# Earlier casts of global values, deferred normalising in slots 1 to 6 and one Strassen unit less at the end of an attention and expert kernel

## The chip, the cores and the metric

The kernel runs on one core of one Trainium2 chip. The metric is device time of one execution in microseconds (us); the figure for a kernel is the median of several runs. One execution is also recorded by the hardware profiler, and the rows in this document come from that record. PE is TensorE, DVE VectorE, ACT ScalarE, POOL GpSimd and SP the queue of SyncE, which issues transfers.

## The reference, cut to what matters

First an attention over 8 batches, 8 heads, 512 local and 32 global positions of width 64, then a layer of 8 experts over all 4352 rows.

```python
s_g = scale * q_g @ concat(k_g, k_l).T          # global rows see every key
out_g = softmax(s_g) @ concat(v_g, v_l)
s_l = concat(q_l @ k_g.T, where(|i-j| <= 32, q_l @ k_l.T, -1e9)) * scale
out_l = softmax(s_l) @ concat(v_g, v_l)         # local rows: a window and the global keys
x = rows of concat(out_g, out_l)                # 4352 x 512
P = exp(x @ w_gate - max), 8 times normalised over rows and columns
out = sum over e of P[:, e] * (relu(x @ w1[e]) @ w2[e])
```

## The kernel before, in words

Each engine works through its own instructions in the order in which the program issues them; there is no scheduler, so the order of the code is the order on each engine. Instructions wait for semaphores that other engines or transfers raise.

**The start and the slots.** A unit n is a batch b and a pair of heads hp (n = 4b + hp; 32 units). The main loop runs slots s = 0 to 33. In slot s the code issues for unit s the scores in three parts, `st_B(s, 0..2)`: products on PE into a score buffer `sc`, then for each block of 64 rows a masking with a running minimum on DVE (`ms`, `mx`, L379) and an exponential on ACT (`Pu`, L382). For unit s-1 it issues the transposes of the window weights (`st_D1`, `ptw` to `pw`), those of the global weights and of the finished rows of unit s-2 (`st_D2`, `tgx` to `pg` and `xT`), and the products with the values, `st_E(s-1)`. For unit s+1 it issues the transposes of keys and queries (`st_A`, `pk` and `pq`, copied to `kTe` by DVE and to `qpl` or `qbd` by ACT). Below, B(s, p), D1(n) and E(n) stand for these calls.

`st_E(n)` multiplies the window weights with the local values in `va` and `vb` (two layouts of the same values, shifted by 64 rows) and the global weights with the global values in `vgz`, into the buffer `po`. It then normalises on DVE: a reciprocal (`rr`, L427) and a product (`xn`, L428). `po` is a single buffer, shared with the scores of the global rows (`st_G1`, `sg`). Slot 2 issues E(0), slot 3 E(1) and E(2), every later slot E(s-1). The global rows follow in `st_G1` (even slots; a maximum `m` on DVE and an exponential `Pg` on ACT), `st_G2`, `st_G3` and `st_G3n` (odd slots; the last normalises: `rg` and `xgn` on DVE and ACT).

`va` and `vb` have a column of ones behind each head's values, and `va` a pad of zeros. For batches 0 and 1 `va` is filled by four loads on POOL's queue and `vb` by one load and by five copies on POOL (`part`, L204 to L209). `vgz` is zero but for the global values and a column `own`; its values are first cast to a scratch `vg16` in DRAM (`cast_vg`, on POOL's queue) and then spread by four transfers on SP's queue (`load_vz`). Ahead of the first slot `clear` sets pad and ones of `va` and `vb` on DVE, and `clear_z` sets `vgz` and `vgn` on POOL. POOL's queue at the start holds, in this order: the loads of queries and keys (`qs`, `ks`) of batch 0, the mask, the cast of the global values, the loads of `va` and `vb`, the cast for batch 1, `clear_z`, the loads of `qs` and `ks` of batch 1, the five copies into `vb`, the first expert weights.

From slot 5 on PE also makes the first two experts' layers in pieces (`p_l1`, `ph` to `hT`; `p_l2`, `py`). Between the transposes of slots 1 to 4 `keep_busy` issues products that nobody reads; they multiply the identity with `kTe`.

**The experts.** The six other experts run in stages with one level of Strassen's scheme: a `Unit` is 256 rows of the second layer with seven products m1 to m7 of 4 instructions each, 28 of 256 columns, in a buffer `z` of which there are two; its sums of inputs (`sums`, four, on DVE), copies on ACT, and reads `r1`, `r2`, `r7` on DVE that add the result into the output rows. The last stage leaves four units u0 to u3. u0 and u3 are done in the plain way, `plain`: for each half j of the rows eight products of 512 columns, then one read; pieces of other units are issued between them at given points `(j, n)`. u1 and u2 are Strassen units; the sums of u2 are formed on POOL.

Of the kernel before, what the change touches and what calls it, by code (L numbers as in the profile page):

```python
# [10 lines left out]
FP16 = mybir.dt.float16  # L11
FP32 = mybir.dt.float32
AF = mybir.ActivationFunctionType
ALU = mybir.AluOpType
# [9 lines left out]
def kernel(  # L24
# [13 lines left out]
    nc = tc.nc  # L38

    B, H, Sl, Dh = q_l.shape  # L40
# [3 lines left out]
    P = 128  # L44
# [5 lines left out]
    NJ = Sl // P  # L50
    HP = H // 2
    DP = D // P
    FT = F // P
# [4 lines left out]
    VW = Dh + 1  # L58
# [10 lines left out]
    ones_f = persist.tile([P, P], FP32)  # L69
    identity = persist.tile([P, P], FP16)  # L70
# [58 lines left out]
    with ExitStack() as att:  # L129
        att_c = att.enter_context(tc.tile_pool(name="att_c", bufs=1))  # L130
        att_in = att.enter_context(tc.tile_pool(name="att_in", bufs=2))
        att_wk = att.enter_context(tc.tile_pool(name="att_wk", bufs=2))
# [45 lines left out]
        def load_vz(b):  # L178
            for i in range(4):
                nc.sync.dma_start(out=vgz[b % 2][i:P:4, i, :, 0:Dh], in_=vg16[b])  # L180

        def cast_vg(b):
            nc.gpsimd.dma_start(out=vg16[b], in_=v_g[b].rearrange("h g d -> g h d"))

        def load_v(b):
            va, vb = vab[b % 2]
            vz = vgz[b % 2]
            src = v_l[b].rearrange("h s d -> s h d")

            def first():  # L190
                if b != 1:
                    cast_vg(b)
                nc.gpsimd.dma_start(out=va[W:P, 0, :, 0:Dh], in_=src[0:96])

            def mid(j):
                nc.gpsimd.dma_start(out=va[:, j, :, 0:Dh], in_=src[P * j - W : P * j + 96])

            def last():
                r = HB if natural(b) else W
                nc.gpsimd.dma_start(out=vb[r : r + W, NJ - 1, :, 0:Dh], in_=src[Sl - W : Sl])  # L200

            def part(eng, lo):
                if lo:
                    eng.tensor_copy(out=vb[96:P, NJ - 1], in_=va[W : 2 * W, 0])  # L204
                    eng.tensor_copy(out=vb[0:HB, 0:2], in_=va[HB:P, 0:2])
                    eng.tensor_copy(out=vb[0:HB, 2:NJ], in_=va[HB:P, 2:NJ])
                else:
                    eng.tensor_copy(out=vb[HB:P, 0:2], in_=va[0:HB, 1:3])
                    eng.tensor_copy(out=vb[HB:P, 2], in_=va[0:HB, 3])  # L209

            def move():
                if natural(b):
                    return part
                nc.sync.dma_start(out=vb[96:P, NJ - 1], in_=va[W : 2 * W, 0])
                nc.sync.dma_start(out=vb[0:W, :], in_=va[HB : HB + W, :])
                nc.sync.dma_start(out=vb[HB : HB + W, :], in_=va[HB + W : P, :])
                nc.sync.dma_start(out=vb[W:HB, 0 : NJ - 1], in_=va[0:W, 1:NJ])
                nc.sync.dma_start(out=vb[HB + W : P, 0 : NJ - 1], in_=va[W:HB, 1:NJ])
                load_vz(b)

            return [first] + [lambda j=j: mid(j) for j in range(1, NJ)] + [last, move]
# [38 lines left out]
        def run(steps):  # L260
            for f in steps:
                f()
# [14 lines left out]
        steps = load_qk(0, 2, 4, H)  # L277
# [12 lines left out]
        def clear(i, eng):  # L290
            va, vb = vab[i]
            eng.memset(va[0:W, 0], 0.0)
            eng.memset(va[:, :, :, Dh:VW], 1.0)
            eng.memset(vb[:, :, :, Dh:VW], 1.0)

        def clear_z(i, eng):
            eng.memset(vgr[i].bitcast(mybir.dt.uint32), 0)
            eng.tensor_copy(out=vgz[i][:, :, :, Dh], in_=own.unsqueeze(2).to_broadcast([P, 4, H]))
            if i == 0:
                eng.memset(vgn[0 : P - Sg], 0.0)  # L300
                eng.memset(vgn[P - Sg : P, :, Dh:VW], 1.0)

        clear(0, nc.vector)
        clear(1, nc.vector)
        for t in range(2):
            (nc.vector.tensor_copy if t else nc.scalar.copy)(out=staged[0][t][:, 0:2], in_=fh[t])
        for a in range(2):
            band = mask[HB * a : HB * (a + 1), 1, 0:KW]
            for base, m, c in ((0, -1, 1), (2 * W, 1, -1)):
                nc.gpsimd.affine_select(out=band, in_=band, compare_op=ALU.is_ge, fill=NEG, base=base,  # L310
                                        pattern=[[c, KW]], channel_multiplier=m)
        run(steps[2:4])
        *steps, move = load_v(0)
        part = move()
        run(steps)
        cast_vg(1)
        clear_z(0, nc.gpsimd)
        load_vz(0)
        nc.sync.dma_start(out=vgn[P - Sg : P, :, 0:Dh], in_=vg16[0])

        st = {}
# [63 lines left out]
        def st_D1(n):  # L385
            d = st[n]
            ptw = ps_tr.tile([P, NHB, P], FP16, tag="tr")
            for i in range(NHB):
                nc.tensor.transpose(ptw[:, i, :], d["Pu"][:, i // 4, 0:KW, i % 4], identity)  # L389
            d["pw"] = att_wk.tile([P, NHB, P], FP16, tag="pw", name="pw")  # L390
            nc.vector.tensor_copy(out=d["pw"], in_=ptw)
# [18 lines left out]
        def st_E(n):  # L410
            b, hp = divmod(n, HP)
            d = st[n]
            vz = vgz[b % 2]
            d["xn"] = att_wk.tile([P, NJ, P], FP16, tag="xn", name="xn")
            po = ps_po.tile([P, NJ, 256], FP32, tag="po")
            for j in range(NJ):
                for a in range(2):
                    for first in (True, False):
                        for par in range(2):
                            i, h = 2 * j + par, 2 * hp + a  # L420
                            lhs, rhs = (d["pw"][:, i], vab[b % 2][par][:, j, h, :]) if first else \
                                (d["pg"][:, i // 4], vz[:, i % 4, h, :])
                            nc.tensor.matmul(po[HB * par : HB * (par + 1), j, VW * a : VW * (a + 1)],  # L423
                                             lhs[:, HB * a : HB * (a + 1)], rhs, start=first, stop=not first)
            pv = po[:, :, 0 : 2 * VW].rearrange("p j (a v) -> p j a v", a=2)
            rr = att_wk.tile([P, NJ, 2], FP32, tag="rr2", name="rr2")
            nc.vector.reciprocal(out=rr, in_=pv[:, :, :, Dh])  # L427
            nc.vector.tensor_tensor(out=d["xn"].rearrange("p j (a v) -> p j a v", a=2), in0=pv[:, :, :, 0:Dh],  # L428
                                    in1=rr.unsqueeze(3).to_broadcast([P, NJ, 2, Dh]), op=ALU.mult)

        gs = {}

# [117 lines left out]
        def keep_busy(n):  # L550
            pm = ps_mm.tile([P, 512], FP32, tag="mm", name="pm")
            for i in range(n):
                nc.tensor.matmul(pm, identity, kTe[0][:, 0:512], start=True, stop=True)

        queue = []
        NU = B * HP
# [5 lines left out]
        def permuted_masks():  # L562
            for i in (3, 2):
                nc.vector.tensor_copy(out=mask[:, i, 0:KW].rearrange("q (y x w) -> q x y w", x=2, w=W),
                                      in_=mask[:, 1, 0:KW].rearrange("q (x y w) -> q x y w", x=2, w=W))
            nc.vector.memset(mask[:, 2, 3 * W : KW], NEG)
        st_A(0)
        unread(2, 256)
        first_keys()
        for s in range(NU + 2):  # L570
# [66 lines left out]
            f1("a")  # L637
            if s < NU:
                st_B(s, 0)
            if even:  # L640
                st_G1(*divmod((s - 2) // 2, 2))
            if 1 <= s <= NU:
                st_D1(s - 1)
            if s == 3:
                st_E(1)
            if g_odd:
                st_G2(gb, gg)
            f2("a")
# [10 lines left out]
            if s < 7:  # L659
                st_A(s + 1)  # L660
            if 1 <= s < 5:
                keep_busy(3)
            if s == 4:
                st_D2(None, 1)
            if s == 1 or s == 2:
# [7 lines left out]
            if s + 1 < NU and s >= 7:  # L673
                st_A(s + 1)
            if s == 2:
                st_E(0)
            if 3 <= s <= NU:
                st_E(s - 1)
            if g_odd:
                st_G3(gb, gg)  # L680
            f2("a")
            if g_odd:
                st_G3n(gb, gg)
            if s == 6:
                f1("v")
# [75 lines left out]
    with tc.tile_pool(name="tpool", bufs=2) as tpool, \  # L761
# [90 lines left out]
        class Unit:  # L852
# [6 lines left out]
            def o(self, j):  # L859
                return acc_of(self.m)[:, self.c[j], :]  # L860

            def sums(self, eng=nc.vector):
                a11, a12, a21, a22 = self.a
                s = self.s = hsum.tile([P, 3, HF, P], FP16, tag="hs", name="hs")
                for o, x, y, op in ((s[:, 1], a11, a21, ALU.subtract), (a21, a21, a22, ALU.add),
                                    (s[:, 0], a21, a11, ALU.subtract), (s[:, 2], a12, s[:, 0], ALU.subtract)):
                    eng.tensor_tensor(out=o, in0=x, in1=y, op=op)  # L867

            def mm(self, o, lhs, rhs, first):
                for fk in range(HF):  # L870
# [247 lines left out]
            w()  # L1118
        u0, u1, u2, u3 = final
        u1.sums()  # L1120
        plain(u0, False, {(0, FT - 2): (x.m3, x.r1, lambda: u2.sums(nc.gpsimd)), (1, 3): (u1.m1,)})
        for w in (u1.m7, u1.m2, u1.m6, u2.m1, u1.m4, u1.m5, u1.r2, u1.r7, u2.m7, u2.m2, u2.m6, u1.m3, u1.r1):
            w()
        plain(u3, True, {(0, 3): (u2.m4, u2.m5, u2.r2, u2.r7), (0, FT - 2): (u2.m3, u2.r1)})


# [28 lines left out]
```

## Time and profile before

| | us |
|---|---|
| runs of the kernel before | 996.26, 996.98, 997.41 |
| median | 996.98 |
| profiled execution | 996.39 |
| its span, first to last instruction | 994.6 |

| stretch of the profiled execution, us | PE busy | DVE busy | ACT busy | POOL busy | granted clock |
|---|---|---|---|---|---|
| 0 to 10 | 6.48 | 7.64 | 4.90 | 9.04 | 1.00 |
| 10 to 20 | 8.56 | 8.37 | 8.93 | 9.68 | 0.83 |
| 20 to 30 | 7.91 | 7.55 | 7.31 | 9.76 | 1.00 |
| 30 to 40 | 7.61 | 7.90 | 9.94 | 9.70 | 1.00 |
| 40 to 50 | 9.76 | 9.11 | 8.85 | 2.35 | 1.00 |
| 50 to 60 | 9.56 | 8.12 | 9.62 | 9.87 | 1.00 |
| 60 to 70 | 10.00 | 7.33 | 8.41 | 0.53 | 1.00 |
| 980 to 995 | 9.04 of 15 | 9.13 | 1.07 | 1.88 | 0.97 |

Each row is a window of the record with the busy time of each engine in it. A granted clock of 1.00 is TensorE at full speed. Slot 2 ends near 22 us, slot 3 near 28, slot 4 near 35, slot 5 near 43, slot 6 near 50.

### The profile page before, as it was taken

Reading aid. Unit: us, or ns where it says so; the run is one execution under the profiler, and the core shown is the slowest. Engines: PE = TensorE matmul, PEld = TensorE weight load, DVE = VectorE, ACT = ScalarE, POOL = GpSimd, SP = SyncE. Lnnn points to the kernel's source line nnn. Section 1 sums busy time; section 2 is a strip of 40 time slices with the busy share of each in tenths; the row PEclk is TensorE's granted clock in tenths of the full one; section 3 lists DMA queues with packets and bytes.
Section 4 is the critical chain, followed back from the end, with each engine's and each line's share of the span. In section 5 each row is a group of like instructions: output and inputs, shape, how many; then the busy total and the mean of one; then the engine's idle time right before and its main releaser. Section 6 shows DMA issues by size and latency. Waiting matters only on the chain.

```text
span 994.6 us, 22109 instructions
## 1 busy us (share of the span) xinstructions
PE 978.8 (98%) x8644; PEld 637.0 (64%) x8644; DVE 776.9 (78%) x1919; ACT 659.8 (66%) x1372; POOL 305.2 (31%) x366
## 2 busy tenths in 40 slices
PE   7899999999999999999999999999999999999997
PEld 5565556555555556666666666676767676766765
DVE  7876666666663755899999888997899999888887
ACT  6898888888884566765555555557765555555551
POOL 9649887887860201111111111101111111100001
PEclk9999999999999999999999999999999999999999
DMA  9999999999952477554443333575654543123043
GB/s 165 189 163 207 226 213 212 224 203 234 225 141 85 121 229 189 161 138 118 117 106 75 75 74 75 138 212 138 160 138 118 117 116 71 38 56 73 2 106 128
DMA packets 138248, 138.65 MB, mean 139 GB/s; under 512 B 56800, under 2 KB 110240, under 8 KB 136096
## 3 DMA queue, kind: packets, MB, share of 16 engines
q0 software_dynamic: 105696, 87.32, 51.6%
q1 hardware_dynamic: 31888, 49.60, 15.7%
q8 instruction: 67, 1.10, 0.4%
q10 hardware_dynamic: 560, 0.33, 0.1%
q14 instruction: 37, 0.30, 0.1%
HBM read 144.46 MB, written 39.58 MB: 185 GB/s over the span
## 4 chain that ended last, share of the span: by engine, by line
PE 93%; DVE 2%; ACT 2%; POOL 1%; DMA 1%; issue 1%; SPq 0%; ACTq 0%; DVEq 0%; POOLq 0%
PE z L871 30%; PE pa L969 18%; PE py L537 12%; PE ph L523 11%; PE pb L969 9%; PE pc L969 4%; PE sc L375 1%; PE po L423 1%; PE ptw L389 1%; ACT Pu L382 1%; PE pk L332 1%; DMA vgz<-vg 1%; PE tgx L399 1%; PE pq L332 1%; PE sg L455 0%
## 5 line engine op out<-in xcount | busy, mean ns | idle before, releaser
L871 PEld LDWEIGHTS <-hs 128*128 128x128 f16 x2320 | 226.1, 98 | 96.1 <-issue 2.9
L871 PE MATMUL z<-w2e,hs 128*128 128x256 f16 x1336 | 200.4, 273 | 2.3 <-DVE o L905 1.0
L871 PE MATMUL z<-v,hs 128*128 128x256 f16 x984 | 147.6, 273 | 0.0
L892 ACT COPY z<-z 128x256 f32<-128x256 f32 x100 | 35.7, 357 | 145.9 <-PE z L871 145.9
L523 PE MATMUL ph<-xT,w1e 128*128 128x512 f16 (+1 forms) x576 | 130.2, 367 | 0.6 <-ACT xT L407 0.6
L537 PE MATMUL py<-w2e,hT 128*128 128x512 f16 x544 | 128.2, 379 | 0.0
L382 ACT ACTIVATE Pu<-ms,mx 128x160 f16<-128x160 f32 x256 | 119.6, 637 | 11.7 <-DVE mx L379 9.6
L969 PEld LDWEIGHTS <-w1e 128*128 128x128 f16 x960 | 87.1, 98 | 51.6 <-issue 1.0
L969 PE MATMUL pa<-t,s 128*128 128x512 f16 x384 | 114.2, 379 | 0.0
L787 POOL DMA_DIRECT2D w1e<-in_moe_w_dram x24 | 17.4, 733 | 290.7 <-PE pa L969 220.4
L379 DVE CUSTOM_DVE_ANT_0 ms<-sc,mask 128x160 f32<-128x160 f32 x256 | 70.0, 320 | 46.3 <-ACT yst L540 27.6
L867 DVE TENSOR_TENSOR hs<-hs 128x512 f16<-128x512 f16 x228 | 99.1, 435 | 8.4
L905 DVE SCALAR_TENSOR_TENSOR oy<-z,lg,oy 128x512 f32<-128x512 f32 x128 | 95.8, 748 | 7.3 <-ACT oy L910 5.9
L787 POOL DMA_DIRECT2D w2e<-in_moe_w_dram x24 | 19.8, 830 | 243.6 <-PE z L871 214.2
L973 DVE CUSTOM_DVE_ANT_0 hx<-pb,s 128x512 f16<-128x512 f32 x96 | 65.9, 686 | 36.4 <-ACT s L1003 30.4
L523 PEld LDWEIGHTS <-w1e 128*128 128x128 f16 x576 | 54.5, 98 | 53.0 <-issue 1.1
L989 ACT ACTIVATE hs<-pa 128x512 f16<-128x512 f32 x96 | 57.2, 596 | 46.8 <-PE pa L969 46.8
L973 DVE CUSTOM_DVE_ANT_0 hs<-pb,s 128x512 f16<-128x512 f32 x96 | 65.8, 686 | 24.1 <-ACT s L1003 23.7
L969 PEld LDWEIGHTS <-s 128*128 128x128 f16 x720 | 65.6, 98 | 28.5 <-issue 0.3
L537 PEld LDWEIGHTS <-hT 128*128 128x128 f16 x544 | 49.9, 98 | 51.9
L528 DVE TENSOR_SCALAR hT<-ph 128x512 f16<-128x512 f32 x58 | 40.1, 691 | 50.1 <-PE ph L523 50.0
L526 ACT ACTIVATE hT<-ph 128x512 f16<-128x512 f32 (+1 forms) x86 | 50.7, 589 | 27.6 <-PE ph L523 27.1
(203 smaller groups left out, 1935.0 us busy)
## 6 DMA issues: line engine op xcount, KB each, us to landing
ys<-yd SPq DMA_DIRECT2D x68, 256.0 KB, 3.2
yd<-yst SPq DMA_DIRECT2D x16, 1024.0 KB, 6.4
pw<-in_moe_w_dram POOLq DMA_DIRECT2D x24, 512.0 KB, 10.1
kept<-psum POOLq DMA_DIRECT2D x24, 512.0 KB, 4.8
s<-kept POOLq DMA_DIRECT2D x12, 768.0 KB, 8.8
v<-kept POOLq DMA_DIRECT2D x12, 768.0 KB, 8.7
w1e<-in_moe_w_dram POOLq DMA_DIRECT2D x12, 512.0 KB, 5.4
w2e<-in_moe_w_dram POOLq DMA_DIRECT2D x12, 512.0 KB, 6.5
```

The lines of the kernel that those rows point to most:

```text
L379: nc.vector.tensor_tensor_reduce(out=ms[:, ii, :], in0=sc[:, SW * ii : SW * (ii + 1)], in1=mask[:, mi, :], scale=-scale, scalar=BIG, op0=A ...
L382: nc.scalar.activation(out=d["Pu"][:, i // 4, :, i % 4], in_=ms[:, ii, :], func=AF.Exp, scale=-1.0, bias=d["mx"][:, i : i + 1])
L523: nc.tensor.matmul(ph[:, 0:n], wts[e][0][:, dk, P * fm : P * (fm + 1)], xT[:, dk, c0 : c0 + n], start=(dk == 0), stop=(dk == DP - 1))
L526: nc.scalar.activation(out=hT[:, fm, 0:n], in_=ph[:, 0:n], func=AF.Relu)
L528: nc.vector.tensor_scalar(out=hT[:, fm, 0:n], in0=ph[:, 0:n], scalar1=0.0, scalar2=None, op0=ALU.max)
L537: nc.tensor.matmul(py, hT[:, fk, P * c : P * (c + 1)], wts[e][1][:, fk, :], start=(fk == 0), stop=(fk == FT - 1))
L867: eng.tensor_tensor(out=o, in0=x, in1=y, op=op)
L871: nc.tensor.matmul(o, lhs[:, fk, :], rhs[:, fk, :], start=(first and fk == 0), stop=(fk == HF - 1), skip_group_check=True)
L905: nc.vector.scalar_tensor_tensor(out=o, in0=z, scalar=p, in1=o, op0=ALU.mult, op1=ALU.add)
L969: nc.tensor.matmul(o, lhs[:, dk, P * f : P * (f + 1)], rhs[:, dk], start=(first and n == 0 and dk == 0), stop=(dk == HD - 1), skip_group_c ...
L973: nc.vector._custom_dve(TENSOR_ADD_SAT, out=self.to(i, j), in0=self.of(ps), in1=self.of(s), s0=BIG, s1=0.0)
L989: nc.scalar.activation(out=self.to(1, 0), in_=self.of(self.pa), func=AF.Relu)
```

## The change

- The cast of the global values of batch 0 (`cast_vg(0)`) is issued ahead of the second pair of loads of `qs` and `ks`. The zeroing of `vgz[0]` moves from POOL to DVE. `clear_z(0)`, now without that zeroing, stands behind the first load of `va`; the rest of `va` and `vb` and the cast for batch 1 follow. `clear(0)` and `clear(1)` move from DVE to POOL, behind those loads.
- `st_E` returns its normalising as a function. In slots 2 to 5 it is kept in `later` and issued in the next slot behind B(s, 0), so that the maskings of the first scores stand ahead of it on DVE; E(1) is normalised at once. In slots 3 and 5 `st_G3n` is kept the same way. In slots 4 and 6 D1(s-1) stands ahead of `st_G1`.
- `keep_busy` issues six products of 256 columns with a tile of ones (`ones_f`, read as 16-bit numbers) in place of three of 512 columns with `kTe[0]`.
- u2 is a plain unit: its sums on POOL go, and the second half of u1 is issued between the products of u2.

```diff
@@ load_v(b), first()
-                if b != 1:
+                if b > 1:
                     cast_vg(b)
...
         def clear_z(i, eng):
-            eng.memset(vgr[i].bitcast(mybir.dt.uint32), 0)
+            if i:
+                eng.memset(vgr[i].bitcast(mybir.dt.uint32), 0)
             eng.tensor_copy(out=vgz[i][:, :, :, Dh], in_=own.unsqueeze(2).to_broadcast([P, 4, H]))
...
-        clear(0, nc.vector)
-        clear(1, nc.vector)
+        nc.vector.memset(vgr[0].bitcast(mybir.dt.uint32), 0)
...
+        cast_vg(0)
         run(steps[2:4])
         *steps, move = load_v(0)
         part = move()
-        run(steps)
+        steps[0]()
+        clear_z(0, nc.gpsimd)
+        run(steps[1:])
+        load_vz(0)
         cast_vg(1)
-        clear_z(0, nc.gpsimd)
-        load_vz(0)
+        clear(0, nc.gpsimd)
+        clear(1, nc.gpsimd)
         nc.sync.dma_start(out=vgn[P - Sg : P, :, 0:Dh], in_=vg16[0])
@@ st_E(n)
-            pv = po[:, :, 0 : 2 * VW].rearrange("p j (a v) -> p j a v", a=2)
-            rr = att_wk.tile([P, NJ, 2], FP32, tag="rr2", name="rr2")
-            nc.vector.reciprocal(out=rr, in_=pv[:, :, :, Dh])
-            nc.vector.tensor_tensor(out=d["xn"]..., in0=pv[:, :, :, 0:Dh], ..., op=ALU.mult)
+            def normalise():
+                (the same four statements)
+            return normalise
@@ keep_busy(n)
-                nc.tensor.matmul(pm, identity, kTe[0][:, 0:512], start=True, stop=True)
+                nc.tensor.matmul(pm[:, 0 : 2 * P], identity, ones_f.bitcast(FP16), start=True, stop=True)
@@ the loop over slots
             if s < NU:
                 st_B(s, 0)
+            for f in later:
+                f()
+            later = []
+            if s in (4, 6):
+                st_D1(s - 1)
             if even:
                 st_G1(*divmod((s - 2) // 2, 2))
-            if 1 <= s <= NU:
+            if 1 <= s <= NU and s not in (4, 6):
                 st_D1(s - 1)
             if s == 3:
-                st_E(1)
+                st_E(1)()
...
             if 1 <= s < 5:
-                keep_busy(3)
+                keep_busy(6)
...
             if s == 2:
-                st_E(0)
+                later.append(st_E(0))
             if 3 <= s <= NU:
-                st_E(s - 1)
+                later.append(st_E(s - 1))
+            if s > 5:
+                run(later)
+                later = []
             if g_odd:
                 st_G3(gb, gg)
             f2("a")
-            if g_odd:
+            if g_odd and s in (3, 5):
+                later.append(lambda gb=gb, gg=gg: st_G3n(gb, gg))
+            elif g_odd:
                 st_G3n(gb, gg)
@@ the end
-        plain(u0, False, {(0, FT - 2): (x.m3, x.r1, lambda: u2.sums(nc.gpsimd)), (1, 3): (u1.m1,)})
-        for w in (u1.m7, u1.m2, u1.m6, u2.m1, u1.m4, u1.m5, u1.r2, u1.r7, u2.m7, u2.m2, u2.m6, u1.m3, u1.r1):
+        plain(u0, False, {(0, FT - 2): (x.m3, x.r1), (1, 3): (u1.m1,)})
+        for w in (u1.m7, u1.m2, u1.m6):
             w()
-        plain(u3, True, {(0, 3): (u2.m4, u2.m5, u2.r2, u2.r7), (0, FT - 2): (u2.m3, u2.r1)})
+        plain(u2, False, {(0, 3): (u1.m4, u1.m5, u1.r2, u1.r7), (1, 3): (u1.m3, u1.r1)})
+        plain(u3, True, {})
```

## The prediction

> **What bounds the kernel now.** Read in this order: the page's busy shares and its chain; the chain of the first 30 us; POOL's timeline up to 21 us; the landing of its loads; the clock by microsecond; DVE's and ACT's timelines around 43 us; PE's waits at the end. All numbers are of one execution of 996.39 us (span 994.6 us). The median of the three runs is 996.98 us, 0.59 us more. A measurement of this kernel tells about 0.2%, or 2 us, from no change.
>
> ```profile
> PE 978.8 (98%) x8644; PEld 637.0 (64%) x8644; DVE 776.9 (78%) x1919; ACT 659.8 (66%) x1372; POOL 305.2 (31%) x366
> PE 93%; DVE 2%; ACT 2%; POOL 1%; DMA 1%; issue 1%; SPq 0%; ACTq 0%; DVEq 0%; POOLq 0%
> ```
>
> PE is the bound. From 59.4 us to 980 us it has no gap that counts, so nothing there moves; only the first 59 us and the last 15 us can. What a part of the start gains or loses in front of the first dense stretch of PE comes out at the end one for one.
>
> ```profile
> 12.30 0.33 POOL vgz L298
> ...
> 14.61 6.71 DMA vgz<-vg
> ...
> 21.36 0.53 PE po L423 x21
> ```
>
> Columns: start, length, what. The chain of the start is POOL's queue, then the transfer of the global values into vgz, then unit 0's products E(0) in slot 2.
>
> ```profile
> 13.15 0.78 POOL L174 DMA_DIRECT2D qs<-in_q_l_dram  x1
> ...
> 16.20 0.61 POOL L204 COPY vb<-va 32x520 f16<-32x520 f16 x1
> ...
> 18.97 1.05 POOL L208 COPY vb<-va 64x1040 f16<-64x1040 f16 x1
> 19.96 0.61 POOL L209 COPY vb<-va 64x520 f16<-64x520 f16 x1
> ```
>
> POOL never idles here. E(0) starts on PE at 20.35, 0.33 us after the copy of L208 that fills the half of vb it reads first, and then waits 0.64 us for vgz. So two things stand level in front of E(0): the transfer of vgz and POOL's copies into vb. E(0) ends at 21.87.
>
> ```profile
> va<-in_v_l_dram POOLq DMA_DIRECT2D x1, 128.0 KB, 7.0
> vb<-in_v_l_dram POOLq DMA_DIRECT2D x1, 32.0 KB, 6.4
> ```
>
> The last column is us from issue to landing: the last load of va (issued 9.04) lands at 16.0, that of vb (9.90) at 16.3.
>
> **Part 1, the start.** vg's cast is issued at 4.4 instead of 5.9, and vgz's ones need POOL only for 0.33 us (L298), at about 7.5. The transfers to vgz can leave at some 10.5 instead of 12.65, and land some 2 us sooner: the 0.64 us wait goes. DVE gives up six memsets (2.50 to 4.33, 1.8 us) for one of 128x1040, by L279 (384 elements, 0.38) about 1.0 us. That is at most 0.2 us, since the first key cast then waits for its load; it is worth nothing in front of E(0), which waits for POOL.
>
> What is late next is POOL. The six memsets of va and vb stand on POOL behind the loads of va and vb. In the changed program as built, the memset of va's ones column waits for all four loads of va, and the next one for vb's load. Before, they ran on DVE at 3 us with nothing to wait for. POOL's new order: vg 0.66, qs 0.77, ks 0.75, first va 0.79, L298 0.33, vgn memsets 0.61 and 0.13, three va 2.65, vb 0.75, vg of b=1 0.59, and va's pad memset at the 0.61 of L300; from 4.37 that ends at about 13.1. Then it waits. The queue of transfers is full from 6 to 21 us (landings follow each other 0.3 to 1.9 us apart) and nothing ahead of va's last load goes away, so it lands about when it did: 16.0 to 16.4. Bounds: 15.2 (issued 10.3, with the 4.9 us of the quickest load of that size) and 17.3 (7.0 us again). I take 16.4. Four column memsets at 0.2 (between the 0.13 of L301 and the 0.33 of L298) and a second pad at 0.61 end at 17.8. Queued behind are four loads (3.05 us) and the five copies: they start at 17.8 where they started at 13.15, 4.65 us later. L208 ends at 24.7, L209 at 25.2, E(0)'s last products 0.3 us after that: 25.5 against 21.87. **+3.7 us** (+2.2 to +5.1 by the two bounds). DVE and ACT have nothing else to do then. The later loads have cover: qs and ks of b=1 land at about 24 and are needed some 29; the first w1e is issued 5 us later but had landed 9 us before its use.
>
> PE idles over 4 us there. The clock says what that costs:
>
> ```profile
> 10.00:11.00 1.00, 0.29 (x12) 0.30 (x12) 0.87 (x4) 1.00 (x4) 1.00 (x2) 0.98 1.88 175
> 12.00:13.00 1.00, 1.00 (x16) 0.63 (x14) 0.95 (x4) 1.00 (x3) 0.94 (x3) 0.50 2.74 150
> ```
>
> First number behind the length: PE's busy time; third from the right: granted clock. After three thin microseconds (0.48, 0.35, 0.29) the clock is 0.50 from 11 to 14.4, and ptw's eight transposes take 1.04 us instead of 0.64. In slot 3 some 1.6 us of PE work (rest of E(0), first scores, E(1), G2) lies on the path; part of it would run at half clock. **+0.3 us**, bounds 0 and 1.6. The Trainium skill (TensorE: Matmul & The Clock Gate, Part 1: The HAM clock gate) says that one idle window of about 3.4 us halves the clock until a busy window has passed; by it the whole 1.6 us would double and the sum below would be 1.3 us more. The row agrees in depth and length, though here PE was thin and not idle.
>
> **Part 2, scores ahead of normalising.** No work is added; DVE's order changes, so gaps decide.
> - Slot 3: before, unit 0's normalising (0.9 us) runs right behind E(0), and E(1), which shares the one po buffer, follows at once (22.90). Now three maskings (0.74) come between, and E(1) with all behind it on PE starts later. ACT's idle 1.18 us before its exponentials shrinks by 0.8, but the slot's second maskings go from 3.07 us behind E(0) to 3.5. +0.45.
> - Slot 4: first scores wait for ACT's qpl copy (27.83); DVE idles for them with the normalising queued behind. ACT does the exponentials earlier, then waits for Pg, whose maximum comes behind normalising. Both cancel: 0.05. Slot 5: 0.1, ACT being full.
> - Slot 6 is the dear one:
>
> ```profile
> 42.60 0.56 DVE L494 TENSOR_SCALAR xgn<-pog,rg 32x64 f16<-32x64 f32 x2
> 43.19 0.69 DVE L528 TENSOR_SCALAR hT<-ph 128x512 f16<-128x512 f32 x1
> 43.91 0.32 DVE L379 CUSTOM_DVE_ANT_0 ms<-sc,mask 128x160 f32<-128x160 f32 x1
> ```
>
> Normalising (41.56 to 43.16) fills the time in which PE makes ph. Moved behind the scores it leaves DVE idle until ph is there (42.6) and adds its 1.6 us after 44.25. G1 waits for po until 45.1, the maximum ends at 47.3 instead of 45.5, Pg follows, and ACT's next exponentials start at about 48.1 instead of 46.43. From there ACT is full until PE waits for it at 58.1. +1.6.
>
> Sum **+2.2 us**. If the gaps of ACT (1.18, 0.84 and 0.81 us) were filled and nothing waited, it would be -1.5; if the pad, pw and G1 waits all add up, +3.0. I take the walk, the nearest to the rows.
>
> **Part 3, unread products.** Six of 256 columns for three of 512: 0.81 us on PE as before. They no longer wait for kTe, which in slot 3 costs PE 0.70 us (25.70 to 26.40). ACT hides it: its queue (Pu, pg, xT, qpl) is busy to 27.83 and takes the next exponentials only then. 0; without that cover -0.7.
>
> **Part 4, the last units.**
>
> ```profile
> PE z L871 <- DVE o L905: 1.0, 1, 1.0
> PE z L871 <- DVE oy L905: 1.0, 1, 1.0
> PE z L871 <- DVE ox L905: 0.3, 1, 0.3
> ```
>
> These are PE's waits from 980 to 990. Measured between issues they are 1.12 (980.54 to 981.66), 0.48 and 1.14 us: 2.74. u2 as a plain unit costs 16 products of 512 at 0.216, 3.46 us, for 28 of 256 at 0.109, 3.05: +0.4. Its first three products cover ACT's copy that u1.m4 waits for; five and three cover r2 and r7 up to 0.1 us. u2's sums leave POOL, and u1's four on DVE go from 4.45 us to 1.7 (0.42 each elsewhere), so x.r1 comes early. The stores stay on SP, and the last goes out after the same three pieces of u3. -2.74 + 0.4 + 0.1 = **-2.2 us** (-2.7 if no wait is left, -1.4 if two of 0.4 us are).
>
> **Sum.** 3.7 + 0.3 + 2.2 + 0 - 2.2 = +4.0: 1000.4 for such an execution, and with the 0.6 us to the median 1001.0.
>
> **Rivals.**
> - *Faster:* POOL's wait is short. Then vgz is what mattered: -0.65 at E(0), -1.0 of ACT's gaps, -2.2 at the end: 996.98 - 3.9 = 993.1. It decides if the last load of va has landed by about 12 us, for then L208 ends by 20.4. For it: the chain names vgz. Against it: the load is issued at 10.3, and 4.9 us is the quickest of its size. 0.13.
> - *No change:* the wait is as I say, but the new order fills ACT's gaps (-1.5) instead of costing 2.2: 3.7 + 0.3 - 1.5 - 2.2 = +0.3, 997.3. For it: ACT's waits for mx (4.9 us in 60). Against it: the walk of slot 6. 0.14.
> - *Slower still:* the half clock covers slot 3, 1.6 us where I took 0.3: 1002.3. This is the rule of the page named above. 0.13.
> - That a part does not do what it says: vgz does land sooner, but only the copies are waited for; this is in the forecast.
>
> **How the numbers follow.** The forecast has 0.60, with a range of its own of 998.5 to 1003.0. Slower: 0.60 + 0.13, and 0.01 of the second rival's spread; same: 0.11 of it; faster: 0.13 and 0.02 of it. The range 996.0 to 1003.8 leaves out the faster rival and the far end of the stall's upper bound.
>
> **What would show it.** POOL idle for 2 to 4 us from about 13 us in front of the memset of va; PE idle 4 us in front of E(0), which ends near 25.5; a clock of 0.5 near 25 to 28; the first dense py near 65.5 instead of 59.4; PE's three waits at the end gone. I am wrong if POOL shows no such wait, if E(0) ends before 23, or if the first py comes less than 4 us later.

## The result

The changed kernel takes 1005.19 us (median; 1004.91 to 1007.39) where the kernel before takes 996.98 on the same chip: 8.2 us more, a ratio of 1.0087 [1.0073, 1.0101]. The forecast was 1001.0, with a range up to 1003.8. The sign was right; the loss is twice the one forecast and lies outside the range. The profiled execution took 1005.11 us, its span 1003.3 (994.6 before).

The page of the changed kernel, its busy shares and the shares of its chain:

```profile
PE 983.8 (98%) x8644; PEld 639.8 (64%) x8644; DVE 773.4 (77%) x1913; ACT 659.6 (66%) x1370; POOL 301.1 (30%) x367
...
PE 94%; ACT 2%; POOL 1%; DVE 1%; DMA 1%; issue 0%; POOLq 0%; DVEq 0%; ACTq 0%
```

PE is busy for 5.0 us more with as many products: twelve more unread ones, each of half the size, and twelve fewer in u2, each of twice the size; u2 adds 0.4 us, the unread ones nothing. Most of the 5.0 us is probably the lower clock: in the first 35 us it is 0.50 for some 17 us, against 3.4 us before, and E(0) takes 1.17 us there, for 0.63 in a kernel below that meets it at full clock. The rest of the 8.7 us is waiting. The chain of waits of the first 30 us (start, length, what) says where the first part is:

```profile
8.27 1.65 POOL va L196 x2
9.92 8.17 DMA va<-in_v_l_dram
...
25.11 1.06 POOL vb L208
26.21 1.17 PE po L427 x28
```

Before, vgz stood in this chain ahead of E(0). Now it is va's last load, issued at 9.92 and landing 8.17 us later, and then POOL's copies. POOL's timeline (start, length, what; in brackets idle time before it and what ended that):

```profile
12.15 0.52 POOL L292 MEMSET va<- 32x520 f16 x1
18.18 0.25 POOL L293 MEMSET va<- 128x32 f16 x1 [5.50 <-DMA va<-in_v_l_dram]
...
22.34 0.61 POOL L204 COPY vb<-va 32x520 f16<-32x520 f16 x1
...
25.11 1.05 POOL L208 COPY vb<-va 64x1040 f16<-64x1040 f16 x1
26.10 0.62 POOL L209 COPY vb<-va 64x520 f16<-64x520 f16 x1
```

POOL stands for 5.50 us at the memset of va's ones column, and the four loads of queries and keys and the five copies stand behind it. The copy of L208 ends at 26.2, 6.1 us later than before. In the waits of PE up to 70 us (engine, tile and line, what it waited for; us in total, times, longest) the same stall and a second kind of wait stand first:

```profile
PE po L427 <- POOL vb L208: 4.1, 1, 4.1
PE sg L462 <- DVE xn L434: 2.7, 2, 1.4
```

The first is E(0); PE was there at 21.9, did its first product and waited 4.1 us. The second is `st_G1` in slots 4 and 6, waiting for a normalising that now stands behind the maskings. The clock by microsecond (PE's busy time first behind the length, granted clock third from the right):

```profile
24.00:25.00 1.00, 0.00 (x0) 0.00 (x0) 0.00 (x0) 0.00 (x0) 1.00 (x2) 0.50 1.11 131
...
28.00:29.00 1.00, 0.94 (x8) 0.67 (x8) 0.89 (x7) 0.52 (x2) 1.00 (x3) 0.50 0.92 68
...
30.00:31.00 1.00, 1.00 (x34) 0.93 (x33) 0.41 (x2) 0.00 (x0) 1.00 (x2) 0.50 1.10 195
```

PE idles at 24 us, and the clock stays at 0.50 from 24 to 34 us, through all of slot 3. DVE's timeline in slot 6, which answers to the three lines around 43 us before:

```profile
51.47 0.69 DVE L535 TENSOR_SCALAR hT<-ph 128x512 f16<-128x512 f32 x1 [0.98 <-PE ph L530]
52.65 0.32 DVE L383 CUSTOM_DVE_ANT_0 ms<-sc,mask 128x160 f32<-128x160 f32 x1 [0.49 <-PE sc L379]
...
53.63 0.69 DVE L434 TENSOR_TENSOR xn<-po,rr 128x512 f16<-128x512 f32 x1
...
54.43 0.56 DVE L501 TENSOR_SCALAR xgn<-pog,rg 32x64 f16<-32x64 f32 x2
```

DVE idles 0.98 us for ph, which the normalising used to cover, and does the normalising behind the maskings. At the end, PE's timeline has u1's second half between the products of u2, and then the rest of u2 and u3 in one piece:

```profile
993.06 1.89 PE L958 MATMUL zp<-w2e,hs 128*128 128x512 f16 x8
994.86 0.60 PE L889 MATMUL z<-w2e,hs 128*128 128x256 f16 x4
995.29 4.74 PE L958 MATMUL zp<-w2e,hs 128*128 128x512 f16 x37
```

No line of these carries a wait, and PE's list of waits from 979 us to the end is empty.

To put the time in its place, the first maskings of some blocks serve as marks. T(s, p) is the start of the first masking of B(s, p) on DVE:

| us | E(0) ends | T(3,1) | T(4,1) | T(5,1) | T(6,1) | T(8,0) | T(8,0) to the end |
|---|---|---|---|---|---|---|---|
| before | 21.9 | 24.9 | 31.9 | 37.5 | 46.1 | 59.2 | 935.4 |
| after | 27.4 | 32.3 | 40.3 | 46.4 | 56.5 | 69.9 | 933.4 |

The start and slots lose 10.7 us. From T(8,0) to the end the kernel gains 2.0.

### The profile page after: what moved, and what is told of

Its sections match the earlier page's. It is cut to its first block, busy times and chain, and to the rows that moved or that the text cites. A ratio compares the mean times of both kernels' runs of the same rounds, so it can differ in the third digit from the quotient of the medians.

```text
span 1003.3 us, 22100 instructions
## 1 busy us (share of the span) xinstructions
PE 983.8 (98%) x8644; PEld 639.8 (64%) x8644; DVE 773.4 (77%) x1913; ACT 659.6 (66%) x1370; POOL 301.1 (30%) x367
## 4 chain that ended last, share of the span: by engine, by line
PE 94%; ACT 2%; POOL 1%; DVE 1%; DMA 1%; issue 0%; POOLq 0%; DVEq 0%; ACTq 0%
PE z L889 30%; PE pa L987 18%; PE py L544 12%; PE ph L530 11%; PE pb L987 9%; PE pc L987 4%; PE po L427 2%; PE sc L379 1%; PE ptw L393 1%; PE zp L958 1%; PE pk L336 1%; DMA va<-in_v_l_dram 1%; ACT Pu L386 1%; PE tgx L403 1%; PE pq L336 1%
## 5 line engine op out<-in xcount | busy, mean ns | idle before, releaser
L889 PEld LDWEIGHTS <-hs 128*128 128x128 f16 x2292 | 223.3, 98 | 93.4 <-DVE hs L885 1.2
L889 PE MATMUL z<-w2e,hs 128*128 128x256 f16 x1320 | 198.0, 273 | 0.0
L386 ACT ACTIVATE Pu<-ms,mx 128x160 f16<-128x160 f32 x256 | 119.6, 636 | 16.7 <-DVE mx L383 14.4
L885 DVE TENSOR_TENSOR hs<-hs 128x512 f16<-128x512 f16 x228 | 96.6, 424 | 8.7 <-DVE hs L885 0.5
```

The costliest lines, as they stand in the source:

```text
L386: nc.scalar.activation(out=d["Pu"][:, i // 4, :, i % 4], in_=ms[:, ii, :], func=AF.Exp, scale=-1.0, bias=d["mx"][:, i : i + 1])
L885: nc.vector.tensor_tensor(out=o, in0=x, in1=y, op=op)
L889: nc.tensor.matmul(o, lhs[:, fk, :], rhs[:, fk, :], start=(first and fk == 0), stop=(fk == HF - 1), skip_group_check=True)
```

## The experiments

The theory: the end gains 2.2 us; the moved clears lose 3 to 6 us by making POOL wait for va's last load; the new order loses 2 to 5; the tile of ones is worth nothing. The rivals: that the new order only lost time because the late start made slot 3 slow; that the early transfers to vgz, not the clears, delay E(0); that the half clock is the larger part. First each of the four parts by itself on the kernel before, which took 997.86 in these four comparisons. Differences in us are between medians; the ratios have their 95% intervals.

**The end alone.**

```diff
-        plain(u0, False, {(0, FT - 2): (x.m3, x.r1, lambda: u2.sums(nc.gpsimd)), (1, 3): (u1.m1,)})
+        plain(u0, False, {(0, FT - 2): (x.m3, x.r1), (1, 3): (u1.m1,)})
...
+        plain(u2, False, {(0, 3): (u1.m4, u1.m5, u1.r2, u1.r7), (1, 3): (u1.m3, u1.r1)})
+        plain(u3, True, {})
```

> Before with only the end changed (u2 plain). Theory A: the three waits of PE at the end (2.74 us between issues) go for 0.4 us more of products, -2.0 to -2.2 us, all of it from 980 us on. Rival B: part of the waits comes back as a wait of u1.m3 for r7 or of u3 for a score buffer, -1.4 us or less. The start shows no difference in either.

Measured: 995.29, ratio 0.9972 [0.9961, 0.9984], 2.6 us less. Within the interval this part does what it was costed at.

**The start alone.**

```diff
-                if b != 1:
+                if b > 1:
...
-        clear(0, nc.vector)
-        clear(1, nc.vector)
+        nc.vector.memset(vgr[0].bitcast(mybir.dt.uint32), 0)
...
+        cast_vg(0)
...
+        clear(0, nc.gpsimd)
+        clear(1, nc.gpsimd)
```

> Before with only the start changed (cast sooner, zeroing on DVE, clears on POOL behind the loads). Theory A: POOL waits 5 to 6 us for va's loads, E(0) ends near 27.4 as in the changed kernel, and slot 3 runs at half clock: +6.5 to +8.5 us. Rival B: the half clock costs little when the order of slots 3 to 6 is the old one, so that only the shift of E(0) is left: +5 to +5.8 us. Rival C: the stall of E(0) is taken up by later gaps: under +3 us.

Measured: 1002.84, ratio 1.0046 [1.0033, 1.0059], 5.0 us more. POOL's timeline and, below it, the first of PE's waits up to 32 us:

```profile
18.98 0.25 POOL L293 MEMSET va<- 128x32 f16 x1 [6.34 <-DMA va<-in_v_l_dram]
```

```profile
PE po L427 <- POOL vb L208: 5.1, 1, 5.1
```

The wait is there without any other part. Behind T(3,1) every step of the slots has its old length (7.0, 5.6, 8.5 and 13.0 us to T(8,0)), so a late start does not by itself make the later slots slow. The half clock lasts from 23.5 to 30.3 us here, and what it costs is small: E(0) takes 1.16 us, and E(0) to T(3,1) 3.35 instead of 3.07. Theory A's 6.5 us and more did not come; the 5.0 us are the low end of rival B.

**The order alone.** `st_E` returns its normalising, kept in `later`; D1 ahead in slots 4 and 6; `st_G3n` kept in slots 3 and 5.

```diff
+            for f in later:
+                f()
+            later = []
+            if s in (4, 6):
+                st_D1(s - 1)
...
-                st_E(0)
+                later.append(st_E(0))
```

> Before with only the order changed (scores ahead of normalising, st_D1 ahead of st_G1). Theory A: DVE waits for ph in slot 5 with normalising queued behind, and Pg comes late in slot 6: +1.5 to +2.5 us, of which +1.6 lies in slot 6. Rival B: ACT's gaps in slots 3 to 5 are filled, and the order costs only where the clock is halved: -0.5 to -1.5 us.

Measured: 1002.38, ratio 1.0054 [1.0035, 1.0074], 4.5 us more, about twice what theory A allowed. One line of PE's timeline, and below it the same wait in PE's list of waits of the kernel before (up to 60 us):

```profile
31.95 0.40 PE L458 MATMUL sg<-kTe,qgT 64*32 64x480 f16 x8 [1.29 <-DVE xn L430]
```

```profile
PE sg L455 <- DVE xn L428: 0.4, 1, 0.4
```

`st_G1` of slot 4 stands 1.29 us for the normalising that shares its buffer, 0.4 before, and PE's queue stands behind it. T(3,1) to T(4,1) takes 7.8 us instead of 7.0, all at a clock of 1.00. T(4,1) to T(5,1) takes 6.4 instead of 5.6, but there the clock is 0.50 from 34.4 to 37.8 us. The loss needs no late start.

**The tile of ones alone.**

```diff
-                nc.tensor.matmul(pm, identity, kTe[0][:, 0:512], start=True, stop=True)
+                nc.tensor.matmul(pm[:, 0 : 2 * P], identity, ones_f.bitcast(FP16), start=True, stop=True)
...
-                keep_busy(3)
+                keep_busy(6)
```

> Before with only the unread products changed (a tile of ones, six of 256 columns). Theory A: the wait of PE for kTe in slot 3 (0.70 us) goes but ACT's queue sets the next step: -0.2 to +0.2 us. Rival B: the wait was on the path: -0.7 us. Rival C: half of the ones tile is zero as 16-bit numbers and the products are shorter, so that the clock falls more often: a lower granted clock between 10 and 30 us and +0.5 us or more.

Measured: 998.0, ratio 1.0001 [0.9992, 1.0009]. The times show nothing, but they leave room for 0.8 us, and the trace has a gain: PE's wait for kTe in slot 3 is gone, and T(3,1) to T(4,1) takes 6.5 us instead of 7.0, with every later step as before.

The parts add to 5.0 + 4.5 + 0.1 - 2.6 = 7.0 us; together they measured 8.2. Next, what in the start costs, with a kernel before at 997.05. The edits of the next three are shown against the start alone.

**The start with the clears left on DVE.**

```diff
         nc.vector.memset(vgr[0].bitcast(mybir.dt.uint32), 0)
+        clear(0, nc.vector)
+        clear(1, nc.vector)
...
-        clear(0, nc.gpsimd)
-        clear(1, nc.gpsimd)
```

> The start of the changed kernel, but the clears of va and vb stay on DVE ahead of the first cast; everything else of before. Theory A: the whole loss of the start is POOL's wait for va's loads; without it the copies into vb end at 20 us or sooner, the transfer to vgz has landed, and E(0) ends at 21 to 21.5: -0.3 to -1.0 us against before. Rival B: the earlier transfer to vgz or the 1.0 us zeroing on DVE costs as well: 0 to +2 us.

Measured: 997.6, ratio 0.9999 [0.999, 1.0008]. POOL's timeline:

```profile
17.38 1.05 POOL L206 COPY vb<-va 64x1040 f16<-64x1040 f16 x1 [0.35 <-DMA va<-in_v_l_dram]
18.49 1.05 POOL L208 COPY vb<-va 64x1040 f16<-64x1040 f16 x1
```

The loss is gone. But the early cast brings nothing either: E(0) starts at 21.4 us, 1.9 after L208's copy ends, with no wait for POOL and none for vgz. What stands ahead of E(0) on PE in slots 0 to 2 sets it.

**The clears on POOL, ahead of va's first load.**

```diff
         run(steps[2:4])
+        clear(0, nc.gpsimd)
+        clear(1, nc.gpsimd)
         *steps, move = load_v(0)
...
         cast_vg(1)
-        clear(0, nc.gpsimd)
-        clear(1, nc.gpsimd)
```

> The start of the changed kernel with the clears on POOL, but ahead of va's first load; everything else of before. Theory A: it is the landing that POOL waits for, not the work of the six memsets; POOL does them in about 1.9 us without a wait and has the zeroing of vgz (1.0 us) less, so the copies into vb end 0.9 to 1.5 us later than before: +0.3 to +1.2 us. Rival B: the memsets themselves, or the later loads, cost what the start cost: +4 us or more.

Measured: 997.1, ratio 0.9998 [0.9989, 1.0007]. POOL does the same six memsets, and in the time they cost nothing that shows: it is their place behind the loads, not the work, that costs the 5 us. The copy of L208 comes 0.9 us later than before (19.90 against 18.97) and E(0) starts at 21.4 all the same.

**The start with the cast in its old place.** The clears stay on POOL behind the loads; the transfers to vgz leave at 12.18 us, near the 12.65 of before, instead of 8.2 to 9.0.

```diff
-                if b > 1:
+                if b != 1:
...
-        cast_vg(0)
         run(steps[2:4])
```

> The start alone with the cast of the global values back in its old place behind qs and ks; clears on POOL behind the loads as in the changed kernel. It tells what makes va's last load land at 18.1 us and not at 16.0. Theory A: the five transfers of 32 KB to vgz and vgn, which now leave at 8 to 11 us, run beside va's loads; with the late cast they leave at 12.5, va's last load lands at 16.5 to 17, POOL's wait is 4.0 to 4.5 us instead of 5.5 to 6.3, and the kernel is 1 to 1.7 us faster than the start alone. Rival B: the load is later because it is issued 0.9 us later behind POOL's small steps; then it lands at 17.5 to 18.5 as before and the kernel is within 0.7 us of the start alone.

Measured: 1002.43, ratio 1.0046 [1.0034, 1.0059]. In the profiled execution (1000.68 us, the lowest of its runs):

```profile
16.45 0.24 POOL L293 MEMSET va<- 128x32 f16 x1 [3.91 <-DMA va<-in_v_l_dram]
```

va's last load lands 6.4 us after issue, where it took 9.0 in the start alone and 8.2 in the changed kernel; in all three it is issued at 9.9, so rival B's later issue is not the reason. PE's wait at E(0) is 2.4 us instead of 5.1. This trace speaks for the early transfers as what delays the load. Two things speak against: the medians do not tell the two kernels apart (both 1.0046), where theory A had 1 to 1.7 us; and with the clears on DVE the transfers leave at 9.70 and va's last load still takes 7.1 us, as before (7.0). What delays the load stays open.

**The changed kernel with more unread products in front of E(0)**, so that PE does not idle in the stall.

```diff
             if s == 2:
+                keep_busy(36)
                 later.append(st_E(0))
```

> The changed kernel with 36 more unread products of 256 columns on PE ahead of E(0), about 4 us of PE work in the time in which PE waits for POOL. Theory A: the half clock from 24 to 34 us comes from PE's idle time ahead of E(0) and costs 1.5 to 2.5 us behind it; with PE busy the clock stays at 1.00 from 22 us on, E(0) takes 0.65 us instead of 1.17, and the kernel is 1.5 to 2.5 us faster than the changed kernel. Rival B: the clock falls all the same, or DVE and ACT set the pace there: within 0.7 us of the changed kernel.

Measured: 1004.77, ratio 1.0069 [1.0055, 1.0083]. The clock by stretch:

```profile
17.00:27.00 10.00, 8.98 (x144) 7.10 (x142) 4.88 (x25) 5.65 (x13) 8.94 (x15) 1.00 0.80 102
27.00:37.00 10.00, 7.41 (x191) 5.83 (x191) 7.60 (x34) 7.11 (x16) 9.35 (x13) 1.00 1.49 155
...
55.00:56.00 1.00, 1.00 (x4) 0.27 (x2) 0.68 (x6) 1.00 (x3) 0.00 (x0) 0.50 1.93 144
```

The half clock of slot 3 is gone, and T(4,1) comes 2.1 us sooner (38.2). But T(8,0) comes only 0.3 sooner (69.6): the clock is 0.50 from 37.0 to 40.4 and from 54.1 to 57.5 instead, behind gaps that the new order makes. E(0) itself started 0.2 us sooner, so the stall's half clock cost about 1.9 us up to T(4,1), and in this trace most of that was lost again later. How much came back over many executions is open: against the kernel before, the medians are 7.7 us more instead of 8.2, the ratios 0.0069 instead of 0.0087, which is 1.8 us, and the intervals overlap.

Last, the new order in pieces, with a kernel before at 997.16. The edits of the next two are shown against the order alone.

**The order only between slots 5 and 6.**

```diff
-                later.append(st_E(0))
+                st_E(0)()
...
-            if s > 5:
+            if s != 5:
                 run(later)
...
-            if s in (4, 6):
+            if s == 6:
```

> Before with the order changed between slots 5 and 6 alone: normalising of E(4) and st_G3n behind the first maskings of slot 6, st_D1 ahead of st_G1 in slot 6. Theory A: DVE idles for ph in slot 5 and Pg and ACT's exponentials come late in slot 6: +1.6 to +2.0 us, nothing ahead of 41 us. Rival B: ACT or PE has slack behind slot 6, under +1 us.

Measured: 999.89, ratio 1.0023 [1.0014, 1.0033], 2.7 us more. T(5,1) to T(6,1) is 10.1 us instead of 8.5: 1.6. In this execution the half clock comes behind the gap, and T(6,1) to T(8,0) takes 14.7 us instead of 13.2. Three windows of a microsecond:

```profile
45.00:46.00 1.00, 0.03 (x4) 0.03 (x8) 0.95 (x5) 0.97 (x3) 0.44 (x1) 1.00 1.22 201
46.00:47.00 1.00, 0.72 (x17) 0.55 (x18) 0.93 (x3) 0.37 (x2) 0.14 (x1) 1.00 1.42 216
47.00:48.00 1.00, 0.70 (x7) 0.70 (x7) 0.97 (x3) 0.25 (x1) 0.00 (x0) 0.50 1.34 210
```

**The order only in slots 3 to 5.**

```diff
-            if s > 5:
+            if s > 4:
                 run(later)
...
-            if s in (4, 6):
+            if s == 4:
```

> Before with the order changed in slots 3 to 5 alone. Theory A: each slot loses on its own, 0.8 us in slot 3 (E(1) waits for po), 0.9 in slot 4 (maskings wait for qpl with normalising behind) and 0.3 to 0.7 in slot 5: +2.0 to +2.5 us, so that this and the run of slot 6 alone add up to the whole order, +4 to +4.5 us. Rival B: the loss of slots 4 and 5 is the half clock that the whole order met at 34.7 us; then +1.0 to +1.5 us where the clock stays at 1.00.

Measured: 999.41, ratio 1.0022 [1.0013, 1.0031], 2.3 us more. The two pieces add to 5.0 us, with 4.5 for the whole order; in ratios it is 0.0045 against 0.0054 [0.0035, 0.0074]. So slots 3 to 5 cost about as much as slot 6. Rival B is not excluded for slot 5: in this trace too the clock is 0.50, from 33.9 to 37.3 us. Slot 4 loses its 0.8 us all but ahead of that, and in the changed kernel slot 5 loses 0.5 us at a clock of 1.00, so only the other 0.4 us of slot 5 can be the clock here.

**The order with the tile of ones.**

```diff
+                later.append(st_E(0))
...
+                nc.tensor.matmul(pm[:, 0 : 2 * P], identity, ones_f.bitcast(FP16), start=True, stop=True)
```

> Before with the order and the unread products changed. Theory A: with the new order the unread products' wait for kTe in slot 3 delays the scores that DVE waits for, so the tile of ones now gains what it did not gain alone: 0.5 to 0.9 us faster than the order alone, +3.3 to +4 us against before. Rival B: ACT's qpl copy still sets the step: within 0.3 us of the order alone.

Measured: 1001.5, ratio 1.0039 [1.0025, 1.0053]. In the trace T(3,1) to T(4,1) is 7.4 us instead of the 7.8 of the order alone, but T(6,1) to T(8,0) is 14.9, with a half clock at 49.6 to 53.1. The intervals of the two overlap: 0.4 us can be seen in the slot, not in the time.

**The end, the early cast with the clears on DVE, the tile of ones, and ten unread products in slot 0.**

```diff
+        plain(u2, False, {(0, 3): (u1.m4, u1.m5, u1.r2, u1.r7), (1, 3): (u1.m3, u1.r1)})
...
+                keep_busy(10)
                 cast_g("qgs")
```

> A version to beat both: before with the plain u2 at the end, the cast sooner with the clears on DVE, the tile of ones, and ten more unread products of 256 columns behind the scores of slot 0, where PE is thin from 9 to 11 us. Theory A: the end gives -2.2 us, and with PE busy at 9 to 11 us the half clock at 11 to 14 us does not come, which gives 0.5 to 1.2 us more: -2.7 to -3.4 us against before. Rival B: the clock falls all the same or the copies of POOL set E(0): -2.0 to -2.5 us as the end alone.

Measured: 995.14, ratio 0.9974 [0.9963, 0.9985]. It beats both kernels, and no more than the end alone does (0.9972). The half clock of the start is still there, from 8.2 to 11.6 us; without the ten products (the start with the clears on DVE) it lasts from 8.0 to 14.8.

## Why the prediction was right or wrong

By marks of the trace, forecast and measured:

| term | forecast | measured | where it is read |
|---|---|---|---|
| E(0) by POOL's wait | +3.7 | +5.0 | E(0) ends at 27.4 for 21.9, less the 0.5 of it that the next row counts |
| half clock behind the stall | +0.3 | +2.2 | E(0) 1.17 us for 0.63 in the order alone; E(0) to T(3,1) 4.9 for 3.8; T(3,1) to T(4,1) 8.0 for 7.4 in the order with the tile of ones |
| new order, slot 3 | +0.45 | +0.8 | E(0) to T(3,1): 3.82 in the order alone, 3.07 before |
| slot 4 | +0.05 | +0.8 | T(3,1) to T(4,1): 7.8 in the order alone, 7.0 before |
| slot 5 | +0.1 | +0.5 | T(4,1) to T(5,1): 6.1 for 5.6 |
| slot 6 | +1.6 | +1.5 | T(5,1) to T(6,1): 10.06 for 8.54 |
| behind slot 6 | 0 | +0.2 | T(6,1) to T(8,0): 13.4 for 13.2 |
| unread products | 0 | -0.4 | T(3,1) to T(4,1): 7.4 with the tile of ones, 7.8 without; alone 1.0001 in the time |
| the end | -2.2 | -2.0 | T(8,0) to the end; alone -2.6 |
| sum | +4.0 | +8.6 | span +8.7 |

The first term is counted against the shown execution of before, in which PE reached E(0) at 20.35 us. In the changed kernel it got there at 21.9 by itself, after a longer half clock in slots 0 to 2, so its wait in the trace is 4.1 us. In the six other traces that have the loads and clears of before, PE got there at 21.1 to 21.7; the forecast was built on an early execution. The first dense product of py came at 70.2 us, where the prediction had about 65.5.

**Right: what POOL waits for.** That the memset of va's ones column waits for va's last load, that the loads and copies behind it start late, and that this holds E(0) is in the trace as written, and the two placements of the clears confirm it: on DVE, or on POOL ahead of the loads, the whole 5 us is gone. The work behind the wait was costed well: 8.3 us from the landing to L208's end, 8.0 measured. The bounds of the term were not: landings at 15.2 and 17.3, 1.2 us before and 0.9 behind the one taken, give +2.5 and +4.6 by the same steps, not +2.2 and +5.1.

**Wrong: the landing of va's last load.** I wrote that "nothing ahead of va's last load goes away, so it lands about when it did: 16.0 to 16.4", with an upper bound of 17.3. It landed at 18.1, 8.2 us after its issue where the forecast had 6.1 and at most 7.0. That step failed. It asked only what goes away ahead of the load, and not what comes beside it. SP's timeline of the changed kernel:

```profile
8.24 2.56 SPq L180 DMA_DIRECT2D vgz<-vg  x4
10.90 0.61 SPq L323 DMA_DIRECT2D vgn<-vg  x1
```

Part 1 itself said that these transfers would leave some 2 us earlier, and priced only their gain. They left 4.4 us earlier (12.65 before), beside va's loads. With the cast in its old place the load took 6.4 us. The Trainium skill (DMA: Bandwidth & Descriptors, Queues, rings and completion order) says that a transfer engine takes turns between the queues that have work, a packet at a time. Transfers beside the load could lengthen it that way; no run here shows the turns. Whether the transfers are the cause stays open, as said under the run with the late cast.

**Wrong in size: the half clock.** The 0.3 us stood on "part of it would run at half clock", with bounds of 0 and 1.6. All of slot 3 did: up to T(3,1) that cost 1.6 us, the price of the rival "slower still", and 0.6 us more in slot 4, together about what the 36 products took away up to T(4,1). The Trainium skill (TensorE: Matmul & The Clock Gate, Part 1: The HAM clock gate) has a window of about 3.4 us, and the trace agrees in what the stall did: three such windows at 0.50 from 24 to 34 us. In slot 4 part of the loss is this clock too, since the window ends only at 34, behind T(3,1). In the start alone there are two, to 30.3, and they cost 0.8 us (0.5 in E(0), 0.3 up to T(3,1)). So with the new order behind it the late start's half clock cost 1.4 us more than without, in these single traces.

**Wrong: slots 4 and 5 of the new order.** "Both cancel: 0.05" balanced ACT's earlier exponentials against its later Pg, and left out PE: G1 shares po with E, so it waits for the moved normalising, and the transposes queued behind it wait too. The row is the 1.29 us ahead of `sg` in the order alone, 0.4 before. What makes the 0.5 us of slot 5 stays open. I had named this wait for slot 6 (where the 1.6 us was right) and for the upper bound of +3.0, and not walked it in slot 4. The order in slots 3 to 5 alone is slower by 0.0022 [0.0013, 0.0031], 1.3 to 3.1 us, where the three terms had 0.6.

**Right: the end.** PE's three waits are gone.

**Right in the time, not in the reason: the unread products.** The 0 rested on "ACT hides it". The times cannot tell 0 from 0.5 us, and three traces show 0.4 to 0.5 us less between T(3,1) and T(4,1): 6.5 for 7.0 alone and in the last version, both with the old order, and 7.4 for 7.8 with the new one. So in these traces ACT did not hide it.

**Why the rivals fell.** The faster one needed vgz to matter. With the clears on DVE it is early and nothing follows: the chain of before named vgz because it came 0.64 us behind PE in an execution in which PE was early. The time for no change needed ACT's gaps to fill; the order alone is slower in every piece. Of "slower still" the mechanism came, at its price of 1.6 us up to T(3,1), and other terms were off beside it.

**What stays open.** The parts add to 7.0 us in medians and 8.2 were measured; the longer half clock in the combination would fit the difference, but the intervals are wide enough for there being none. Whether the early transfers make any of the 5 us of the start is not shown.

## What to carry to other kernels

Before an instruction is moved behind a load on a queue, look at whether it touches the load's target: here a clear of columns beside the loaded ones waited 5.5 us for the landing, and everything queued behind it waited too. When a transfer is made to leave sooner, look also at what it now runs beside, and not only at what it frees; here a landing taken as unchanged came 1.7 us late, though whether those transfers caused it was not shown. Where a step is moved behind others on one engine, walk the single buffer that it reads in every slot, up to the engine that wants that buffer next.

## What the runs showed of the hardware

- **Small transfers beside a large load: not settled.** From issue to landing, va's last load of 128 KB took 6.7 to 7.6 us in the seven kernels with the start of before, whose five transfers of 32 KB on SP leave at 12.6 us or later. Where these leave at 8.2 to 9.7 us it took 9.0, 8.2 and 7.8 us with the clears behind the loads (the start alone, the changed kernel, the 36 products), but 7.1, 6.9 and 7.6 us with the clears elsewhere (on DVE, ahead of the loads, the last version). With the clears behind the loads and the transfers at 12.18 us it took 6.4.
- **Thin microseconds can bring the half clock, but how thin does not decide it.** It lasted about 3.4 us or multiples of that. Ahead of it PE was busy for 0.48, 0.35 and 0.29 of a microsecond (before, at 11 us), 0.24, 0.34 and 0.42 (36 products in front of E(0), at 54) and 0.55, 0.03 and 0.72 (order between slots 5 and 6, at 47). But 0.00, 0.63 and 0.42 (the changed kernel, from 53 us), 0.00, 0.61 and 0.42 (the order alone, from 47 us) and 0.91, 0.00 and 0.92 (the order alone, from 9 us) brought none. With one gap filled it came at the next: with the 36 products at 37 us instead of 24.
- **The same start differs by about 1 us between executions.** The kernel with only the end changed has the start of before, but its half clock covers 10.1 to 17 us where the shown one of before covers 11 to 14.4, and its T(8,0) is 60.2 instead of 59.2. A start read from one execution is not known to better than that.
